# A fused local-attention, Fourier-mixing and MLP kernel on one core: global keys inside the score blocks of two batches, a second MLP in seven products from its third chunk on, and a rebuilt opening

## Chip, core and metric

The kernel runs on one core of one Trainium2 chip. The metric is device time in microseconds (us) of one execution; a kernel's time is the median of several runs. TensorE (PE) does matmuls into PSUM, VectorE (DVE) and ScalarE (ACT) drain PSUM and do elementwise work, GpSimd (POOL) does small work and issues DMAs that cast, SyncE (SP) issues the other DMAs.

## What is computed

Input q, k, v are (4 batches, 8 heads, 768 tokens, 64). Attention keeps, for each query, the local keys 0 to 95 tokens back and the 8 global keys (tokens 0 to 7), with a linear distance bias. Its output x, (4, 768, 512), goes through a Fourier mixing and a two-layer MLP:

```
scores = q k^T / sqrt(64) - slope[h] * dist     # dist = 96 for a global key out of reach
keep   = (key < 8) or (0 <= query - key < 96)
x      = softmax(scores where keep) v           # heads side by side: (4, 768, 512)
u      = x + real(fft2(x))                      # over tokens and features
un     = (u - mean(u)) / sqrt(var(u) + 1e-6)
out    = u + relu(un @ w_ch1) @ w_ch2           # 512 -> 2048 -> 512
```

## The kernel before

Work is float16 with float32 sums. Each of the four batches goes through the same stages, and the stages of different batches are interleaved on the engines.

*Attention* is done by head pair (`hp`, 4 per batch). q and k are loaded and cast by POOL's DMA queue (`load_qk`, L418), v by `load_v` (L404). In batches 0 and 1 PE transposes them (`trans`, L506, matmul L521) and DVE or ACT copies the result out (L528, L532); in batches 2 and 3 the DMA does it (`trans_dma`). `score` (L539) makes a block of scores for two blocks of 128 keys by up to 256 queries each. A head pair needs three such blocks (g = 0, 1, 2), for both heads at once, one on each half of PE's rows. In batches 0 and 1 the bias is added by PE (L565) and ACT's exp writes the weights (L599). In batches 2 and 3 each block is four matmuls with 128 output rows (L571), ACT takes the exp (L596) and DVE multiplies by a mask (`mul`, L611). The 8 global keys have a block of their own per batch (`glob`, L634, matmul L644, exp L654 into `EG`). In `av` (L665) the weights multiply V (L687); for queries beyond the second block of 128, a further matmul per head adds the global part from `EG` and a small copy `vG` of the global V rows (L680). DVE divides by the sum (`norm`, L704 and L706).

*Mixing.* DVE folds the tokens by symmetry (`fold_s`, for batch 0 `fold_0`, L803, by head pair) and the features (`fold_d`, L874); PE multiplies by tables of cosines and sines (`y_unit`, L927 into `py`; `u_unit`, L1016 into `pu`). The DVE adds x back and sums for the mean (`evac`; batch 0: `evac0`, L1038). In batches 1 to 3, x comes back in the needed token order through DRAM (`bounce`). In batch 0, PE brings it into that order with a permutation matrix, `spread` (L991): 12 matmuls of 512 columns per chunk, whose results go to PSUM in strides of four columns, in the same PSUM tile as `pu`.

*MLP.* A chunk c = 3b + pr is 256 tokens, twelve chunks in all. `centre` (L1092) makes un; PE or the DMA transposes it (`nt_unit`, L1141; `nt_dma`). `ph_unit` (L1161) is the first layer: 8 units of 16 matmuls, 256 columns each, per chunk (L1171), drained by ACT (L1177) or DVE (L1178) with the relu. The second layer has two forms. For c below CS = 8, `pg_unit` (L1193): 32 matmuls of 512 columns (L1204), two DVE drains (L1213). From CS on, `pg_units` (L1281): the chunk is taken as a 2 by 2 block product (two groups of 128 tokens, two halves of the hidden width, two halves of the output), done with seven block products instead of eight, 56 matmuls of 256 columns (L1288). For that DVE forms four sums of the hidden blocks per chunk (`s_sums`, L1248) and, once, four sums of blocks of w_ch2 (`w2_sums`, L1234), and drains the products in five steps (L1306). The products p1, p45, p6, p32, p7 wait for their sums and for each other's drains, since p1, p6, p7 share one PSUM tile and p45, p32 another.

*Order.* The order of instructions on each engine is fixed when the kernel is built, by a planner (`Plan`, L23): it keeps an estimated time per engine, and always issues the unit or operation that could start first, changed by a table of offsets (`BIAS`). All engines then work through their lists in order, waiting on semaphores. Buffers are named by tag and reused (`NBUF`): "hT", the hidden activations, has 3.

*Opening.* While the first loads run, PE does 18 warm-up matmuls (L1429). Then batch 0's attention starts; before a head pair's first score block, 4 filler matmuls are issued (`FILL`, L549).

Of the kernel before, what the change touches and what calls it, by code (L numbers as in the profile page):

```python
# [17 lines left out]
class Ring(str):  # L18

    k = 0  # L20


class Plan:  # L23
# [8 lines left out]
    LAND = {("c", "id"): 3.0, ("ld", 0): 4.8, ("ld", 1): 5.0, ("c", "dist"): 6.3, ("c", "gb"): 6.5}  # L32
    LAT = {"ACT": 0.14, "DVE": 0.12, "POOL": 0.08}

    def __init__(self):
        self.t = {"PE": 0.0, "ACT": 0.0, "DVE": 0.0, "POOL": 0.0, "SP": 0.7, "DMA": 6.0, "DMA2": 1.0}
        self.tok = {}
        self.ready = []
        self.pending = []
        self.rings = {}  # L40
        self.left = {}
        self.n = 0
        self.lanes = [0.0] * 8
        self.soft = [0.0] * 8
# [24 lines left out]
    def later(self, ways, needs=(), after=0.0, outs=(), uses=(), ring=None, lat=0.0, dma=0.0, then=None, rank=1, nd=None):  # L69

        self.n += 1
        if nd is None:
            nd = 0 if dma == 0 else 1 if ways[0][0] in ("SP", "ACT") else -1
        self.pending.append((self.n, ways, list(needs), after, outs, uses, ring, lat, dma, then, rank, nd))
        self.promote()
# [11 lines left out]
    def first(self):  # L87

        best = None
        for i, (ready, p) in enumerate(self.ready):  # L90
            if p[11]:
                ready = [max(r, self.lane(p[11])) for r in ready]
            c = (min(max(self.t[w[0]], r) for w, r in zip(p[1], ready)) - self.AHEAD * (p[10] < 0) + self.bias(p[4][0] if p[4] else None),
                 p[10], ready[0], p[0], i)
            if best is None or c < best:
                best = c
        return best
# [11 lines left out]
    def emit(self, place):  # L109
# [8 lines left out]
        if dma:  # L118
            q = "DMA2" if outs and outs[0] in (("ld", 0), ("ld", 1), ("ld", 2), ("ld", 3), ("c", "id"), ("c", "dist"), ("c", "gb")) else "DMA"
            end = self.t[q] = max(self.t[q], end) + dma  # L120
        else:
            lat += self.LAT.get(eng, 0.0)
        for o in outs:
            self.tok[o] = max(end + lat, self.LAND.get(o, 0.0)) if dma else (end + lat, eng)
        for u in uses:
            self.used(u, end + lat)
        lanes = self.lanes if nd > 0 else self.soft
        for _ in range(abs(nd)):
            lanes.append(max(end + lat, self.t[eng] + 2.2, *[self.LAND.get(o, 0.0) for o in outs]))
            lanes.pop(0)  # L130
        if ring is not None:
            self.rings[ring].append((end + lat, ring.k))
        if then is not None:
            then(end + lat)
        self.promote()

    def lane(self, nd):
        return self.lanes[nd - 1] if nd > 0 else self.soft[-nd - 1]

    narrow = False  # L140

    def pe(self, us, after=0.0, narrow=False):
        if narrow != self.narrow:
            us += 0.1
        self.narrow = narrow
# [3 lines left out]
    def slot(self, tag):  # L149
# [7 lines left out]
    BIAS = {('kG', 3): 3, (1, 2): 0.7, ('s', '*', 8): 0.3, ('mk1', '*', 2): 0.7, ('h', 1, 3): 0.3, ('v', 3, 2, 0): 6,  # L157
            ('w', '*', 1): 0.7, ('qk', 11, 0, 0): 0.7, ('ss', 1, 0): -1.5, ('ob', '*', 7): -3,
            ('qk', 14, 1, 0): -0.7, ('vGh', 3, 3): 3, (2, '*', 8): -0.7, ('vGh', 1, 3): -0.3, ('vGh', 3, 0): -0.3,
            ('xb', 12, 1): 6, ('qk', 13, 1, 0): 3, (3, '*', 1): 1.5, ('xb', '*', 2): 0.3, ('ss', 5, 1): -0.7,  # L160
            ('ss', '*', 7): -0.7, ('u', '*', 5): 0.3, (1, 5): -3, ('h', 0, 7): -3, ('ss', '*', 8): 0.7,
            ('h', '*', 2): 3, ('w2t', '*', 1): 0.3, ('qkT', 14): 1.5, ('h', '*', 10): 1.5, ('un', '*', 3): 1.5,
            ('mk1', 0): 0.3, ('un', '*', 2): -0.3, ('mk1', 5): -1.5, ('un', 5, 1): 1.5, ('ex', 2, 2, 2): -1.5,
            ('u', '*', 8): -0.7, (2, 3): -3, ('er', '*', 3): 0.7, ('qkT', '*', 2): -3, ('qk', 9, 1, 0): 3,
            ('un', 8, 1): 0.3, ('qk', 14, 1, 1): -3, (2, 56): -0.3, ('mk1', '*', 7): 0.7, (1, 86): -0.3,
            ('er', 16): 3, ('ob', '*', 10): 0.7, ('h', '*', 7): -1.5, ('ob', '*', 14): 3, ('un', 6, 1): -0.3,
            ('ex', 1, 2, 1): -3, ('unT', 0): -0.7, ('h', 0, 0): -0.7}
    AHEAD = 0.0
# [7 lines left out]
    FILL = 4  # L176
# [3 lines left out]
    def run(self, streams):  # L180

        left = [[(*u, (i, k)) for k, u in enumerate(s)] for i, (s, _) in enumerate(streams)]
        while True:
# [20 lines left out]
            if op is not None and (best is None or op[0] <= best[0]):  # L204
# [5 lines left out]
            elif not any(left) and not self.pending:  # L210
# [27 lines left out]
def kernel(  # L238
# [24 lines left out]
    DM = ()  # L263
    assert (B, H, S, Dh, NG, NL) == (4, 8, 768, 64, 8, 96)
# [18 lines left out]
    distk = np.concatenate([np.where(near < far, rel, np.where(key < NG, NL, far)), near, near[:, 0:P]], 1)  # L283
# [64 lines left out]
    NBUF = {"hT": 3, "qk": 4, "qkT": 4, "er": 2, "eg": 1, "x": 1, "xr": 1, "zy": 1, "eA": 1,  # L348
# [12 lines left out]
    dist_sb = kon.tile([P, 2, NM], FP16, tag="dist", name="dist")  # L361
    dist_k = kon.tile([P, NM], FP16, tag="distk", name="distk")
    sid = kon.tile([P, H, P], FP16, tag="sid", name="sid")
# [5 lines left out]
    W2 = {}  # L369
    mhalf = kon.tile([P, 2], FP32, tag="mhalf", name="mhalf")  # L370
    zero = kon.tile([P, 1], FP32, tag="zero", name="zero")
# [4 lines left out]
    vG = [kon.tile([P, HP, 2, 66], FP16, tag=f"vG{i}", name=f"vG{i}") for i in range(2)]  # L376

    EG = kon.tile([P, 2, 512], FP16, tag="eg", name="eg")
# [15 lines left out]
    def swq(fn, cost, needs, outs, dma, fifo=True):  # L394
        after = []
        then = None
        if fifo:
# [3 lines left out]
            then = lambda t: pl.tok.__setitem__(("sw", k), pl.t["POOL"])  # L401
        pl.later([("POOL", cost, fn)], needs + after, 0.0, outs, lat=2.2, dma=dma, rank=0, then=then)

    def load_v(b, hp):  # L404
        h0 = 2 * hp
        if b >= FB:
# [3 lines left out]
            swq(whole, 1.0, [("avdone", b - 2), ("wl", 7)], [("v", b, hp, t) for t in range(2)], 1.5, False)  # L410
            return
        for t in range(2):
# [3 lines left out]
            swq(run, 0.75, ([("avdone", b - 2), ("wl", 7)] if b > 1 else []), [("v", b, hp, t)], 0.7, b < 2)  # L416

    def load_qk(b, hp):  # L418
        n = HP * b + hp
        h0 = 2 * hp  # L420
        tag, ti = ("hT", n // 2) if n < 6 else ("qk", n - 6)
        for w, src in enumerate((q, k)):
            if b >= FB:
                for h in range(2):
# [4 lines left out]
                    swq(run, 0.75, free(tag, ti) + [("wl", 7)], [("qk", n, w, h)], 0.75, False)  # L429
# [7 lines left out]
            if n in pl.HW:  # L437
# [3 lines left out]
                pl.later([("ACT" if w else "SP", 0.45, read)], [], 0.0, [("ld", w + n)], lat=1.7, dma=1.35)  # L441
# [11 lines left out]
            swq(run, 0.82, free(tag, ti), [("qk", n, w)], 1.1)  # L453
# [13 lines left out]
    pl.users(("C",), 4 * HP + 2 + HP + len(YG) // 2 + NP + 1 - 3)  # L467
    pl.users(("D",), 4 * HP + 2 + HP + len(YG) + NP + 1)
# [16 lines left out]
    def kg_copies(b, hp):  # L485
        n = HP * b + hp

        def cp(on):
            on.tensor_copy(kG[b % 2][:, hp, :].rearrange("p (m t) -> p t m", t=2),
                           TT[n][:, 1, 0:P].rearrange("p (t m) -> p t m", t=2)[:, :, 0:16])  # L490
        pl.later([("POOL", 0.25, lambda: cp(nc.gpsimd)), ("DVE", 0.12, lambda: cp(V))], [("qkT", n)], 0.0,
                 [("kG", n)], [("free", "qkT", n)], rank=RA(b))

    def trans_dma(b, hp):
        n = HP * b + hp

        def xb(w):
            if n not in TT:
                TT[n] = buf("qkT", n, [P, 2, S], FP16, 4)
            nc.sync.dma_start_transpose(TT[n][:, w].rearrange("p (j x) -> p j x", x=P), qk16[n][:, w].rearrange("p i h d -> p (i h d)"))  # L500
        for w in range(2):
            pl.later([("SP", 1.3, lambda w=w: xb(w))], [("qk", n, w, h) for h in range(2)] + (free("qkT", n) if w == 0 else [("xb", n, 0)]), 0.0,
                     [("xb", n, w)], lat=1.7, dma=1.25)
        pl.later([("SP", 0.0, lambda: None)], [("xb", n, w) for w in range(2)], 0.0, [("qkT", n)], [("free", "qk", n - 6)])

    def trans(b, hp):  # L506
# [4 lines left out]
        src_at = ("hT", n // 2) if n < 6 else ("qk", n - 6)  # L511

        def run(start, ring):
# [9 lines left out]
            e = pl.pe(1.0, start, True)  # L523
            pl.used(("free",) + src_at, e)

            def evac():
                TT[n] = buf("qkT", n, [P, 2, S], FP16, 5)
                V.tensor_copy(TT[n], pt[:, :, 0:S])  # L528

            def evac_act():  # L530
                TT[n] = buf("qkT", n, [P, 2, S], FP16, 5)
                A(TT[n], pt[:, :, 0:S], AF.Copy)  # L532
            pl.later([("DVE", dve2(2 * S), evac)] * (n not in pl.AQ) + [("ACT", act(2 * S), evac_act)] * (b < 2), free("qkT", n), e, [("qkT", n)], CD(b, ring) * (b == 0), ring=ring, rank=RA(b))
            kg_copies(b, hp)
# [4 lines left out]
    def score(b, hp, g):  # L539
# [3 lines left out]
        def run(start, ring):  # L543
# [4 lines left out]
            for _ in range(pl.FILL if b == 0 and g == 0 else 0):  # L548
                nc.tensor.matmul(pa[:, 0, :], idn, dist_sb[:, 0, 0:512], start=True, stop=True, skip_group_check=True)  # L549
            w0, w1_ = ((256, CO), (CO, CO), (256, P))[g]  # L550
# [16 lines left out]
            for i, c0, cw in tiles:  # L567
                for s in range(2):
                    lo = 64 * s
                    if b >= FB:  # L570
                        nc.tensor.matmul(pa[:, s, c0:c0 + cw], TT[n][lo:lo + 64, 1, i * P:i * P + P],  # L571
                                         TT[n][lo:lo + 64, 0, i * P:i * P + cw], start=True, stop=True)
# [6 lines left out]
            e = pl.pe(0.27 + 0.28 * pem, start, True)  # L579
# [4 lines left out]
            def cut(t):  # L584

                if g == 1:
                    return t.rearrange("p s (i c) -> p s i c", i=2)[:, :, :, 0:CO]
# [16 lines left out]
            def mul():  # L604
                h = slice(2 * hp, 2 * hp + 2)
                o = cut(expst[hp][:, :, g * 512:g * 512 + (384 if g == 2 else 512)])
                if g == 1:
                    m = mk[:, h, 256:256 + CO].unsqueeze(2).to_broadcast([P, 2, 2, CO])
# [7 lines left out]

    def v_global(b):
        for hp in range(HP):
# [961 lines left out]
```

## Time and profile before

| | us |
|---|---|
| median of 3 runs | 256.53 (256.25 to 256.71) |
| the profiled execution | 257.17 |
| its span, first to last instruction | 255.4 |

The profile shows the one execution of 257.17 us. All times in views are microseconds from the start of its span. Busy time is the time covered by an engine's records; a matmul's record goes on past the start of the next one, so the cost of a matmul in a row of equal ones is taken from the distance of starts. In a group's row stand line, engine, operation, what is written from what, count, busy time, mean in ns of one, and the engine's idle time just before with what ended it. The windows view gives, for each stretch, its length and the busy time of PE, weight load, DVE, ACT and POOL, then the granted clock, the DMA share and GB/s.

### The profile page before, as it was taken

The page shows a single profiled execution, that of the slowest core. Times are in us where ns is not written, and L with a number is a line of the kernel's source. Part 1 is how long each engine was busy: PE and PEld are TensorE (multiplying, and loading weights), DVE is VectorE, ACT ScalarE, POOL GpSimd, SP SyncE. Part 2 cuts the span into 40 slices and gives each one's busy share as a digit, 9 for nine tenths or more (in the row PEclk, how much of TensorE's full clock was granted, in tenths as well). Part 3 has the DMA queues.
Part 4 walks back from the last instruction along what each step waited for, and adds up shares of the span by engine and source line. Part 5 has one row for each costly group of instructions (what it writes and reads, how often), then busy time and mean ns, then how long its engine had stood idle before and what let it go on. Part 6 is the DMA issues. An engine that isn't in the chain of part 4 may idle for free.

```text
span 255.4 us, 6779 instructions
## 1 busy us (share of the span) xinstructions
PE 244.0 (96%) x2838; PEld 176.2 (69%) x2838; DVE 172.0 (67%) x413; ACT 140.5 (55%) x237; POOL 89.0 (35%) x127
## 2 busy tenths in 40 slices
PE   7998687999999999999999999999999999999994
PEld 2565465498768754677794475688886577888883
DVE  4539589556995317668669879788997434674563
ACT  3477899785686321699736144953567334433200
POOL 8788734208967428556001001110022104010010
PEclk9999999999999999999999999999999999999999
DMA  7999999995999999989995704312331621130213
GB/s 197 167 165 181 276 206 175 184 167 36 167 180 194 170 172 187 220 103 81 145 124 159 201 3 123 86 41 44 129 120 42 83 41 49 53 108 0 83 47 120
DMA packets 93502, 32.11 MB, mean 126 GB/s; under 512 B 81728, under 2 KB 90048, under 8 KB 93472
## 3 DMA queue, kind: packets, MB, share of 16 engines
q0 software_dynamic: 66272, 17.06, 67.1%
q1 hardware_dynamic: 23904, 11.54, 22.5%
q10 hardware_dynamic: 3296, 3.08, 4.0%
q8 instruction: 22, 0.36, 0.6%
q14 instruction: 8, 0.07, 0.1%
HBM read 31.54 MB, written 8.65 MB: 157 GB/s over the span
## 4 chain that ended last, share of the span: by engine, by line
PE 89%; DVE 7%; ACT 2%; issue 1%; ACTq 0%
PE ph L1171 33%; PE pg L1204 22%; PE pgD L1288 6%; PE pgA L1288 4%; PE pav L687 4%; PE py L927 3%; PE pu L1016 3%; PE pz L1429 3%; PE sc L571 3%; PE pt L521 2%; ACT ex L599 2%; PE pav L680 1%; PE sc L549 1%; PE pu L991 1%; DVE qkT L528 1%; DVE x L706 1%
## 5 line engine op out<-in xcount | busy, mean ns | idle before, releaser
L1171 PE MATMUL ph<-unT,w 128*128 128x256 f16 x768 | 92.5, 273 | 0.0
L1171 PEld LDWEIGHTS <-w 128*128 128x128 f16 x768 | 72.9, 98 | 13.2 <-issue 2.5
L1177 ACT ACTIVATE hT<-ph 128x512 f16<-128x512 f32 x77 | 45.7, 598 | 46.9 <-PE ph L1171 46.5
L1204 PE MATMUL pg<-w,hT 128*128 128x512 f16 x256 | 60.4, 379 | 0.0
L1204 PEld LDWEIGHTS <-hT 128*128 128x128 f16 x256 | 24.4, 98 | 24.3 <-issue 0.9
L596 ACT ACTIVATE er<-sc 128x992 f16<-128x992 f32 (+2 forms) x24 | 21.7, 929 | 9.8 <-DVE ex L611 6.4
L599 ACT ACTIVATE ex<-sc 128x992 f16<-128x992 f32 (+2 forms) x24 | 20.7, 928 | 5.7 <-PE sc L575 5.5
L1213 DVE SCALAR_TENSOR_TENSOR u<-pg,sm,u 128x512 f32<-128x512 f32 x16 | 12.0, 747 | 14.9 <-PE pg L1204 14.8
L1117 POOL TENSOR_SCALAR sm<-sm 128x2 f32<-128x2 f32 x12 | 2.9, 242 | 53.8 <-ACT un L1110 53.8
L1110 ACT ACTIVATE un<-un 128x512 f16<-128x512 f16 x24 | 14.9, 624 | 8.3 <-DMA unT<-un 6.6
L611 DVE TENSOR_TENSOR ex<-er,mk 128x992 f16<-128x992 f16 (+2 forms) x24 | 14.7, 625 | 5.9 <-ACT er L596 5.9
L1178 DVE TENSOR_SCALAR hT<-ph 128x512 f16<-128x512 f32 x19 | 13.0, 688 | 7.8 <-PE ph L1171 7.7
L687 PE MATMUL pav<-v,ex 128*128 128x65 f16 x352 | 17.3, 193 | 0.0
L428 POOL DMA_DIRECT2D qk<-in_q_dram x16 | 13.6, 864 | 8.5 <-DMA qkT<-qk 4.8
L740 POOL DMA_INDIRECT xr<-xd,back x3 | 4.0, 1338 | 35.6 <-DVE ex L611 17.2
L687 PEld LDWEIGHTS <-ex 128*128 128x128 f16 x352 | 15.8, 97 | 0.6
L1101 ACT ACTIVATE un<-u,sm 128x512 f16<-128x512 f32 x11 | 7.8, 720 | 14.4 <-DVE sm L1083 10.0
L414 POOL DMA_DIRECT2D v<-in_v_dram x16 | 12.1, 766 | 7.2 <-DMA w<-in_moe_w_ch_dram 5.6
L428 POOL DMA_DIRECT2D qk<-in_k_dram x16 | 13.6, 862 | 1.9 <-DMA v<-in_v_dram 1.7
L680 PE MATMUL pav<-vG,eg 128*128 128x65 f16 x128 | 14.2, 193 | 0.0
L941 ACT ACTIVATE zy<-py 128x1024 f16<-128x1024 f32 (+1 forms) x13 | 10.3, 827 | 6.8 <-PE py L927 6.5
L1288 PEld LDWEIGHTS <-hT 128*128 128x128 f16 x128 | 12.5, 98 | 1.8
(152 smaller groups left out, 394.9 us busy)
## 6 DMA issues: line engine op xcount, KB each, us to landing
w<-in_moe_w_ch_dram POOLq DMA_DIRECT2D x8, 512.0 KB, 11.5
out_dram<-u SPq DMA_DIRECT2D x15, 256.0 KB
v<-in_v_dram POOLq DMA_DIRECT2D x16, 96.0 KB, 7.4
qk<-in_q_dram POOLq DMA_DIRECT2D x16, 96.0 KB, 5.4
qk<-in_k_dram POOLq DMA_DIRECT2D x16, 96.0 KB, 6.2
v<-in_v_dram POOLq DMA_DIRECT2D x8, 192.0 KB, 13.1
xr<-xd SPq DMA_DIRECT2D x3, 512.0 KB
xd<-x ACTq DMA_DIRECT2D x2, 768.0 KB
```

The lines of the kernel that those rows point to most:

```text
L428: nc.gpsimd.dma_start(qk16[n][:, w, :, h], src[b, h0 + h].rearrange("(i m) d -> m i d", m=P))
L596: A(mine(), cut(pa), AF.Exp, 0.0, 0.125)
L599: A(cut(expst[hp][:, :, g * 512:g * 512 + (384 if g == 2 else 512)]), cut(pa), AF.Exp, 0.0, 0.125)
L611: VT(o, mine(), m, op=ALU.mult)
L680: nc.tensor.matmul(o[:, s * 65:(s + 1) * 65], EG[:, s, (j - 2) * P:(j - 1) * P], vG[b % len(vG)][:, hp, s, 0:65], start=True, stop=False, ...
L687: nc.tensor.matmul(o[:, s * 65:(s + 1) * 65], lhsT, v16[b % 2][:, 2 * hp + s, i, 0:65], start=(j < 2 and a == 0), stop=(a == len(ops) - 1) ...
L1110: A(x, x, AF.Square, accum_out=MV[c][:, a, 2:3])
L1171: nc.tensor.matmul(ph[:, a * CH:(a + 1) * CH].rearrange("p (x m) -> p x m", x=2), W1[0][:, d, jb * P:(jb + 1) * P], UNT[c][:, :, d, :], st ...
L1177: pl.later([("ACT", act(512), lambda: A(dst, ph, AF.Relu)), ("DVE", dve(512), lambda: V.tensor_scalar_max(dst, ph, 0.0))], [], e, [("h", c ...
L1178: ("DVE", dve(512), lambda: V.tensor_scalar_max(dst, ph, 0.0))],
L1204: nc.tensor.matmul(pg, HT[c][:, jb, t * P:(t + 1) * P], W2[0][:, jb, :], start=(jb == 0), stop=(jb == NJ - 1))
L1288: nc.tensor.matmul(o, lhs(j), rhs(j), start=(first and j == 0), stop=(j == NK - 1), skip_group_check=True)
```

## The change

Three things change, and the planner's order with them.

1. **Global keys of batches 2 and 3.** The separate global block, its exp and its matmuls in `av` go. In a score block, the second 128 queries never use key rows 0 to 31 of that block (they are 97 or more tokens back). These 32 rows now get the scores of keys 0 to 31 of the whole sequence, and the mask keeps the first 8. To place them, each block is made from pieces of 32 keys, in PE tiles of 64 by 32 (`tile_position=(lo, 32 * a)`): 18 or 20 matmuls instead of 4. V needs the same exchange: `v_back` copies blocks 1 to 4 of V to `vB` and writes rows 0 to 31 from block 0 (POOL or DVE).

```diff
-                        nc.tensor.matmul(pa[:, s, c0:c0 + cw], TT[n][lo:lo + 64, 1, i * P:i * P + P],
-                                         TT[n][lo:lo + 64, 0, i * P:i * P + cw], start=True, stop=True)
+                        for a in range(4):
+                            for k0, q0, q1 in ([(i * P + 32 * a, 0, cw)] if a or i == 0 else [(i * P, 0, P)] + [(0, P, cw)] * (cw > P)):
+                                nc.tensor.matmul(pa[32 * a:32 * a + 32, s, c0 + q0:c0 + q1], TT[n][lo:lo + 64, 1, k0:k0 + 32],
+                                                 TT[n][lo:lo + 64, 0, i * P + q0:i * P + q1], start=True, stop=True, tile_position=(lo, 32 * a))
...
+    def v_back(b, hp):
+        def cp(eng):
+            h = slice(2 * hp, 2 * hp + 2)
+            eng.tensor_copy(vB[hp], v16[b % 2][:, h, 1:NS - 1, :])
+            eng.tensor_copy(vB[hp][0:32], v16[b % 2][0:32, h, 0:1, :].to_broadcast([32, 2, NS - 2, 66]))
...
-                        if j >= 2:
+                        if j >= 2 and b < FB:
                             nc.tensor.matmul(o[:, s * 65:(s + 1) * 65], EG[:, s, (j - 2) * P:(j - 1) * P], vG[b % len(vG)][:, hp, s, 0:65],
...
+                            w = vB[hp][:, s, i - 1, 0:65] if b >= FB and a and i else v16[b % 2][:, 2 * hp + s, i, 0:65]
```

2. **Seven products from chunk c = 2 on** (the third). For c = 2 to 7 the sums lie in memory that other stages leave free (`EG`, `vG`), one buffer each, and the third sum overwrites the second, so it waits for product 6; the first sums of a chunk wait for products of the chunk before. One sum of w_ch2 blocks is written in place in w_ch2, after the last `pg_unit` of chunks 0 and 1. "hT" has 2 buffers, and one more ("tt") is shared by loads, batch 1's x and sums of w_ch2.

```diff
-    CS = 8
+    CS = 2
+    LATE = 8
...
         def s4():
-            VT(new(2), block(0, 1), SX[c, 1], op=ALU.subtract)
+            if lean:
+                SX[c, 2] = SX[c, 1]
+                VT(SX[c, 2], block(0, 1), SX[c, 1], op=ALU.subtract)
...
+            if lean:
+                return [("sA", c - 1) if i == 0 else ("sB", c - 1)] if c > CS else [("avdone", 1), ("free", "eg", 1)]
...
+    NBUF = {"hT": 2, "tt": 1, ...
```

3. **Opening of batch 0.** The filler matmuls go. For head pairs 1 and 3 the token fold is done by PE (`fold_pe`: 32 matmuls of 128 columns with plus or minus identity as weights) and copied out by ACT or DVE. `spread` becomes a unit of its own, in plain column order, into a PSUM tile of its own, copied to u by ACT or DVE; `evac0` then adds `pu` to it. The small copies of global keys go to the engine that copies the transposed q and k. The planner gets a model of the DMA queues and a new table of offsets, so that the order of all engines changes: batch 0's attention now comes wholly ahead of batch 1's transposes, and the permutation and the two tables are loaded ahead of batch 1's q and k.

```diff
-            for _ in range(pl.FILL if b == 0 and g == 0 else 0):
-                nc.tensor.matmul(pa[:, 0, :], idn, dist_sb[:, 0, 0:512], start=True, stop=True, skip_group_check=True)
...
+        def fold_pe(hp):
+                for n, terms in enumerate(ZS):
+                    o = pf[:, n // 4, (n % 4) * P:(n % 4 + 1) * P]
+                    for x, (w, i) in enumerate(terms):
+                        nc.tensor.matmul(o, w, X[0][:, i, cols], start=(x == 0), stop=(x == len(terms) - 1))
...
-                        nc.tensor.matmul(pu[64 * h:64 * h + 64, a, :].rearrange("p (r n) -> p n r", r=4), PX[0][t, 3 * (r // 2) + jj],
-                                         X[0][t, 3 * hx + jj].rearrange("p (n r) -> p n r", r=4), start=(jj == 0), stop=False,
+                        nc.tensor.matmul(px[64 * h:64 * h + 64, a, :], PX[0][t, 3 * (r // 2) + jj], X[0][t, 3 * hx + jj], start=(jj == 0), stop=(jj == 2),
                                          skip_group_check=True, tile_position=(64 * (r % 2), 64 * h))
```

The table shows instructions that come and go, counted in both kernels.

| | before | after |
|---|---|---|
| PE: score matmuls of batches 2 and 3 | 96 | 448 |
| PE: second-MLP matmuls, 512 / 256 columns | 256 / 224 | 64 / 560 |
| PE: attention times V, global / rest | 128 / 352 | 64 / 352 |
| PE: fold / filler | 0 / 16 | 64 / 0 |
| DVE: sums of hidden blocks | 16 | 40 |
| DVE: drains of the second MLP | 37 | 55 |
| POOL / DVE: copies for `vB` | 0 / 0 | 12 / 4 |

## The prediction, made before the changed kernel was run

> **What bounds the kernel now.** I read the page first: engine shares, slices, shares of the chain.
>
> ```profile
> span 255.4 us, 6779 instructions
> ...
> PE 244.0 (96%) x2838; PEld 176.2 (69%) x2838; DVE 172.0 (67%) x413; ACT 140.5 (55%) x237; POOL 89.0 (35%) x127
> ...
> PE   7998687999999999999999999999999999999994
> ...
> DVE  4539589556995317668669879788997434674563
> ...
> DMA  7999999995999999989995704312331621130213
> GB/s 197 167 165 181 276 206 175 184 167 36 167 180 194 170 172 187 220 103 81 145 124 159 201 3 123 86 41 44 129 120 42 83 41 49 53 108 0 83 47 120
> ...
> PE 89%; DVE 7%; ACT 2%; issue 1%; ACTq 0%
> ```
>
> TensorE (PE) is 96% busy and carries 89% of the chain. Only the opening (first seven slices of 6.4 us) and the last slice are not full. So the kernel is a sum of matmul time behind an opening. The DVE row shows the danger: slices 21 to 30 stand at 7 to 9. The windows view says how much room is left there.
>
> ```profile
> 0.00:42.00 42.00, 34.70 (x654) 21.24 (x658) 27.96 (x102) 29.28 (x40) 28.38 (x45) 1.00 1.59 198
> 103.00:135.00 32.00, 32.00 (x446) 24.48 (x445) 22.38 (x43) 23.30 (x40) 11.01 (x16) 1.00 1.26 126
> 135.00:162.00 27.00, 27.00 (x187) 14.23 (x184) 23.37 (x57) 12.06 (x16) 3.08 (x5) 1.00 0.46 125
> 162.00:200.00 38.00, 38.00 (x421) 29.98 (x420) 32.37 (x63) 22.71 (x40) 5.87 (x10) 1.00 0.30 74
> ```
>
> The columns after the length are PE, weight load, DVE, ACT, POOL. From 103 to 200 us PE never idles although DVE is 70 to 87% busy; the granted clock is 1.00 throughout. In the first 42 us PE is idle for 7.3 us.
>
> **The change part by part.** Prices come from the chain in order of time, where a piece lasts from its start to that of the next.
>
> ```profile
> 8.74 0.97 PE sc L549 x4
> 10.58 0.81 PE pt L521 x24
> 47.21 1.41 PE pu L991 x12
> 81.50 0.89 PE pu L1016 x16
> 91.97 9.50 PE pg L1204 x44
> 103.68 0.38 PE ptu L1141 x32
> 105.91 0.32 PE sc L571 x4
> 106.23 1.85 PE ph L1171 x16
> 108.08 0.31 PE sc L571 x4
> 120.77 0.34 PE pgl L644 x8
> 124.67 0.27 PE sc L571 x4
> 181.00 8.73 PE ph L1171 x80
> 240.29 1.75 PE pgD L1288 x16
> ```
>
> *Second MLP.* A 512-column matmul costs 9.50/44 = 0.216 us, a 256-column one 8.73/80 = 0.109, and the seven-product code already in use (L1288) pays the same, 1.75/16. A chunk goes from 32 x 0.216 = 6.91 to 56 x 0.109 = 6.11 us; six chunks (c = 2 to 7): **-4.8 us**. Beyond its last chunk nothing hides PE, so this counts in full, if DVE keeps up (below).
>
> *Global keys.* Each switch between matmul shapes costs about 0.10 us (16 ph matmuls: 1.85 next to a score, 1.75 otherwise). Batches 2 and 3 lose one global-score block each, 0.34 plus a switch: -0.9. They also lose 64 of their 240 attention-times-V matmuls; 60 such lie between these rows of the timeline:
>
> ```profile
> 125.76 0.35 PE L687 MATMUL pav<-v,ex 128*128 128x65 f16 x6
> 127.57 1.91 PE L1171 MATMUL ph<-unT,w 128*128 128x256 f16 x16
> ```
>
> so 1.81/60 = 0.030 us each: **-1.9**. On the other side the 96 score matmuls become 448 narrow ones of 32 keys. Before, a head pair's three score blocks cost 0.32 + 0.31 + 0.27 = 0.90 us: two row halves at once, 512 columns in a row. Eight places could work at once now, so the least is the same time (+0.2 for eight pairs: 256 instead of 240 columns). But in the corner that holds the global keys two 128-column pieces follow each other on one place, and if what stands behind them waits, a block costs up to 0.12 us more: 24 blocks, +2.7. No row shows two matmuls in a row on one narrow place; I take the middle, **+1.5**.
>
> The page "TensorEngine Tiling (Array Packing)" of the Trainium skill, section Performance Considerations, speaks against the split: each matmul has an overhead of about 60 cycles, which as an estimate is 25 ns a piece and 448 x 25 ns = 11 us in all. The row L1141 above disagrees: 32 small matmuls in 0.38 us with the switch, 9 to 12 ns each.
>
> *Opening, on PE.* The 16 filler matmuls go (4 in 0.97): -3.9. The three spreads lose their strided columns; in plain order they should run like the four 496-column matmuls of the first row below, 0.24 us for each four:
>
> ```profile
> 17.48 0.40 PE L565 MATMUL sc<-dist,sid 64*64 64x496 f16 x4
> 17.72 0.38 PE L575 MATMUL sc<-qkT 64*64 64x256 f16 x8
> ```
>
> Twelve cost 0.74 instead of 1.41: -2.0. The fold of head pairs 1 and 3 on PE adds 64 matmuls at 0.89/16: +3.6. PE work in all: -4.8 - 0.9 - 1.9 + 1.5 - 3.9 - 2.0 + 3.6 = **-8.4 us**.
>
> *Opening, idle time.* These timeline rows are batch 0's path: first and last exps, the second global exp, the last attention-times-V, the first mixing matmul.
>
> ```profile
> 10.30 2.62 ACT L599 ACTIVATE ex<-sc 128x992 f16<-128x992 f32 x3 [2.54 <-PE sc L575]
> 23.42 2.56 ACT L599 ACTIVATE ex<-sc 128x992 f16<-128x992 f32 x3 [0.84 <-PE sc L575]
> 31.04 1.26 ACT L654 ACTIVATE eg<-pgl,gb 64x512 f16<-64x512 f32 x2 [0.59 <-PE pgl L644]
> 34.28 0.22 PE L687 MATMUL pav<-v,ex 128*128 128x65 f16 x2
> 42.81 1.91 PE L927 MATMUL py<-t,ww 128*128 128x256 f16 x16 [0.37 <-DVE ww L899]
> ```
>
> The exps of batch 0 ended at 25.98, but the second global exp ran at 31.04: a transpose copy and three exps of batch 1 stood ahead of it on ACT. The changed order puts batch 0's 12 exps and both global exps first, with no transpose copy between. ACT needs 4 x 2.6 + 2 x 1.26 = 12.9 us from 10.30; I allow one more for gaps, so the last attention-times-V ends near 24.7, not 34.5. From there to the first mixing matmul it was 8.5 us; two of four DVE folds go, a PE fold with its copies and a 1024-wide copy of the spread come in, and I keep the 8.5, and add 0.8 for late loads (below). The first mixing matmul comes near 34.0 instead of 42.81. Counted by the prices above, PE work ahead of it falls from 33.9 to 28.3 us (seven of batch 1's 12 score blocks, not all, stand ahead), so idle time there falls from 8.9 to 5.7: **-3.2**. Bounds: 0 (the loads hold everything) to -5. The spread's copies then crowd DVE and ACT before the first ph: +0.7 (0 to 2).
>
> Queues: on POOL's queue three tables, 0.9 MB, now stand ahead of batch 1's q and k, which come up to 5 us later by the GB/s row (slices 2 to 4, 165 to 276). PE takes their transpose ahead of the fold, near 25 us, when they land or up to 2 us before: hence the 0.8. On SP ident falls behind q, back and one vgs load; what it feeds still waits for the warm-up matmuls.
>
> *DVE.* This is what the gain is paid with. Rows by shape:
>
> ```profile
> L1261 DVE TENSOR_TENSOR mk<-hT 128x1024 f16<-128x1024 f16 x4 | 2.8, 690 | 1.0 <-ACT hT L1177 0.8
> L1306 DVE SCALAR_TENSOR_TENSOR u<-pgD,sm,u 128x512 f32<-128x512 f32 x7 | 5.3, 750 | 8.7 <-PE pgD L1288 8.7
> L1306 DVE SCALAR_TENSOR_TENSOR u<-pgA,sm,u 128x256 f32<-128x256 f32 x8 | 3.8, 480 | 2.8 <-PE pgA L1288 1.6 <-POOL sm L1118 1.1
> L1213 DVE SCALAR_TENSOR_TENSOR u<-pg,sm,u 128x512 f32<-128x512 f32 x16 | 12.0, 747 | 14.9 <-PE pg L1204 14.8
> ```
>
> Per chunk: four sums of 0.69 and 2 x 0.48 + 3 x 0.75 us of drains come, 2 x 0.75 go: +4.5, less some 0.4 by which neighbouring records overlap. Six chunks: +25 us on 172.0; the opening's edits about cancel. I summed both engines' rows over the changed order, from chunk 5's transpose to the last mixing drain of batch 3: PE 75.5 us, DVE 73.7. DVE goes from 86% (same stretch before) to **98%** of PE's time. New waits sit in its queue: the fourth sum of a chunk waits for product 6, since it overwrites that product's operand, and each chunk's first sums wait for the last chunk's products; behind them stand exps times mask, norms and mixing drains, for which PE waits. On POOL, masked copies of V wait for the previous batch's last use, with rstd and the gather behind. hT has two buffers, not three. At 98% some of this must surface; I take **+4.0 us** (0 if DVE never waits; 8, if it reaches only the 90% of its busiest slices).
>
> The sum against the profiled execution (257.17 us around a span of 255.4): -8.4 - 3.2 + 0.7 + 4.0 = -6.9, so 250.3. The runs' median, 256.53, is 0.64 below the profiled execution, so the median after: **249.6 us**.
>
> **The rivals.**
> *DVE sets the middle.* 73.7 us at 86%, what it reached before, is 85.7: 10.2 us over PE's 75.5 instead of 4, total 255.8; I put the case at 252 to 256. For: 98%. Against: at 87% in 135 to 162 us PE lost nothing.
> *The opening gives nothing:* loads hold batch 1's part, idle stays 8.9: 252.8. For: the DMA row is full up to slice 9, 57 us. Against: batch 0's own loads do not move.
> *POOL copies stop the DVE.* Six of eight V copies go to POOL:
>
> ```profile
> L963 POOL COPY rev<-zy x2: 390/393/396, 153.1 to 194.6; 128x256 f16<-128x256 f16 x2
> ```
>
> A copy of 528 elements at that rate takes 0.8 us; twelve, if each held DVE up, 9.7 us into a stage with 2 us of slack, of which my 4 us count half: 249.6 + 9.7 - 2 - 2 = 255.3. The skill's "SBUF — State Buffer", section SBUF: two separate sides, states that rule: DVE with two SBUF inputs and GpSimd share a port pair under an exclusive lock. Against: no DVE row of before is stretched next to a POOL copy.
> *Slower: handoffs.* In the seven-product chunks c = 2 to 7, PE meets four points per chunk where the next product waits for a DVE sum or drain just queued. If PE stands there for one full DVE operation, 0.75 us, 24 times, that is 18 us instead of my 4: 263.6. It decides from (6.9 + 4.0)/24 = 0.45 us a handoff on. Against: chunks 8 to 11 have the same handoffs and run without a gap, though beside a DVE at half load.
> *Narrow pieces paid one by one:* at the 0.033 us of L521, 448 cost 14.8 instead of about 6.3: 258.1.
>
> **How the numbers follow.** Forecast 0.62 (245 to 252). DVE sets the middle 0.15, opening 0.08, POOL copies 0.04, narrow pieces 0.03, handoffs 0.08. With every unknown at its good end (scores +0.2, DVE 0, opening -5) it is 242.5; I go to 244. Upwards the range takes in the opening's case and most of DVE's: 255. Left out: some 0.15 above, a few hundredths below. About 0.2% (0.5 us) is what a measurement here can tell from no change. Slower: handoffs and narrow pieces, 0.11; within: 0.02 of DVE's case; faster: the rest, 0.87.
>
> **What would show it.** First py near 34; last batch-0 pav near 25. Score blocks of batches 2 and 3: 0.31 a piece is no split cost, 0.42 the corner wait, over 0.6 the one-by-one rival. Seven products at 1.75 for 16. DVE over 90% from 110 to 190 us, with PE idle after DVE at pgA and pgD of a few us. I am wrong if PE idles over 8 us there, or if py starts after 38.

## The result, and the profile after

| | before | after | ratio, 95% interval |
|---|---|---|---|
| median of 6 runs each, one chip | 256.39 us (256.14 to 256.81) | 253.94 us (253.19 to 254.79) | 0.9907 (0.9883 to 0.9932) |
| the profiled execution / its span | 257.17 / 255.4 us | 253.83 / 252.0 us | |
| first mixing matmul (py) | 42.81 us | 39.7 us | |
| from there to the end of the span | 212.6 us | 212.3 us | |

The kernel is 0.93% faster; the forecast had 2.7%. The page of the changed kernel: busy times, then PE, DVE and granted clock in 40 slices of 6.3 us, then the shares of the chain.

```profile
span 252.0 us, 7702 instructions
...
PE 237.1 (94%) x3302; PEld 192.8 (77%) x3302; DVE 195.2 (77%) x445; ACT 139.5 (55%) x228; POOL 99.9 (40%) x137
...
PE   7783898899999999999999999979999999999994
...
DVE  2636799795889869798899989976799987646183
...
PEclk9998899999999999999999999999999999999999
...
PE 81%; DMA 6%; DVE 6%; ACT 4%; issue 1%; SPq 1%; ACTq 0%
```

PE's busy time fell by 6.9 us, but the span by 3.4 only: idle time was added. The fourth slice (19 to 25 us) stands at 3, and the clock at 8 in it and in the next. A DMA share of 6% is new in the chain. The chain in order of time (start, length, what) says which DMAs these are at the opening:

```profile
2.25 5.25 DMA ident<-idm
...
15.04 5.41 DMA vgs<-in_v_dram
20.48 0.22 DVE vG L704
20.73 0.67 DVE vG L704
21.46 0.56 DVE x L784
22.05 0.22 DVE vG L704
22.30 0.97 DVE qkT L589
23.31 0.40 PE sc L638 x8
```

and the timeline of the same kernel, in square brackets the idle time before each row and what ended it, shows who stood:

```profile
20.48 0.92 DVE L704 CAST vG<-vgs 8x128 f16<-8x128 f32 x2 [5.46 <-DMA vgs<-in_v_dram]
...
23.31 0.40 PE L638 MATMUL sc<-qkT 64*64 64x240 f16 x8 [3.67 <-DVE qkT L589]
...
30.03 0.22 PE L764 MATMUL pav<-v,ex 128*128 128x65 f16 x2
...
39.70 1.92 PE L1035 MATMUL py<-t,ww 128*128 128x256 f16 x16
...
10.97 2.56 ACT L662 ACTIVATE ex<-sc 128x960 f16<-128x960 f32 x3 [4.05 <-PE sc L638]
...
23.76 0.97 ACT L662 ACTIVATE ex<-sc 128x960 f16<-128x960 f32 x1 [3.44 <-PE sc L638]
26.27 1.26 ACT L729 ACTIVATE eg<-pgl,gb 64x512 f16<-64x512 f32 x2 [1.54 <-PE pav L756]
```

Read it from the first row on. DVE stands 5.46 us for a load of `vgs`: 4 KB, the global rows of V. The two casts after the wait belong to **batch 1** (L704); a matmul first uses what they write at 62.54 us, some 40 us later. Behind them in DVE's queue, which works in order, stand batch 0's first norm (L784) and the copy of its fourth q and k (L589). So PE waits 3.67 us, ACT 3.44, and the last attention-times-V of batch 0 ends at 30.25 instead of near 25. The load itself could not be issued earlier: all four heads' rows of a batch land in one buffer `vgs`, and batch 1's loads (L697) wait until batch 0's casts have read it, 15.0 us.

The stretches in which the forecast feared DVE (columns: length, PE, weight load, DVE, ACT, POOL, clock, DMA share, GB/s):

```profile
0.00:34.00 34.00, 26.00 (x465) 17.48 (x466) 19.38 (x73) 17.90 (x24) 25.95 (x40) 0.95 1.64 191
110.00:135.00 25.00, 24.65 (x455) 20.70 (x454) 23.02 (x46) 14.59 (x23) 11.78 (x17) 1.00 0.94 116
135.00:162.00 27.00, 26.99 (x339) 23.49 (x338) 25.84 (x62) 14.31 (x24) 6.25 (x10) 1.00 0.60 118
162.00:190.00 28.00, 26.42 (x416) 22.77 (x414) 22.68 (x41) 17.02 (x29) 2.12 (x4) 1.00 0.44 91
```

DVE is 92% and 96% busy from 110 to 162 us, near the forecast, and 81% from 162 to 190. But PE idles 0.36 us in the first two stretches, and 1.58 in the third. The waits view of PE from 40 to 250 us (total, times, longest) names that last one, and it is not DVE:

```profile
PE ph L1270 <- DMA unT<-un: 1.5, 1, 1.5
PE ptu L1240 <- ACT ex L662: 0.7, 1, 0.7
PE pav L764 <- DVE ex L674: 0.3, 1, 0.3
PE sc L626 <- DVE zy L1051: 0.2, 1, 0.2
```

### The profile page after: what moved, and what is told of

Read it like the earlier page. It is cut to its first block, busy times and chain, and to the rows that moved or that the text cites. A ratio compares the mean times of both kernels' runs of the same rounds, so it can differ in the third digit from the quotient of the medians.

```text
span 252.0 us, 7702 instructions
## 1 busy us (share of the span) xinstructions
PE 237.1 (94%) x3302; PEld 192.8 (77%) x3302; DVE 195.2 (77%) x445; ACT 139.5 (55%) x228; POOL 99.9 (40%) x137
## 4 chain that ended last, share of the span: by engine, by line
PE 81%; DMA 6%; DVE 6%; ACT 4%; issue 1%; SPq 1%; ACTq 0%
PE ph L1270 33%; PE pgD L1413 13%; PE pgA L1413 10%; PE pg L1303 6%; PE pav L764 4%; PE py L1035 4%; PE pu L1123 3%; DMA unT<-un 2%; DMA vgs<-in_v_dram 2%; PE sc L634 2%; DMA ident<-idm 2%; ACT ex L662 2%; DVE qkT L589 1%; PE pf L943 1%; PE pt L582 1%; ACT zy L1049 1%
## 5 line engine op out<-in xcount | busy, mean ns | idle before, releaser
L1413 PEld LDWEIGHTS <-hT 128*128 128x128 f16 x320 | 30.8, 98 | 4.2
L659 ACT ACTIVATE er<-sc 128x1024 f16<-128x1024 f32 (+1 forms) x24 | 22.5, 954 | 5.9 <-PE sc L634 5.0
L662 ACT ACTIVATE ex<-sc 128x960 f16<-128x960 f32 (+2 forms) x24 | 20.9, 923 | 8.1 <-PE sc L638 8.0
L1431 DVE SCALAR_TENSOR_TENSOR u<-pgA,sm,u 128x256 f32<-128x256 f32 (+1 forms) x30 | 17.1, 569 | 7.5 <-PE pgA L1413 6.6
L1431 DVE SCALAR_TENSOR_TENSOR u<-pgD,sm,u 128x512 f32<-128x512 f32 (+1 forms) x21 | 15.1, 721 | 8.5 <-PE pgD L1413 8.4
L674 DVE TENSOR_TENSOR ex<-er,mk 128x1024 f16<-128x1024 f16 (+1 forms) x24 | 15.5, 658 | 3.3 <-ACT er L659 3.3
L1287 POOL DMA_INDIRECT out_dram<-u,back x4 | 4.8, 1196 | 32.4 <-DVE u L1431 30.3
L1303 PE MATMUL pg<-w,hT 128*128 128x512 f16 x64 | 15.0, 379 | 0.0
L638 PE MATMUL sc<-qkT 64*64 64x240 f16 (+2 forms) x192 | 9.0, 260 | 4.5 <-DVE qkT L589 4.4
L784 DVE TENSOR_TENSOR x<-pav,rc 128x384 f16<-128x384 f32 x24 | 12.6, 554 | 0.6
```

What stands on the lines that cost most here:

```text
L659: A(mine(), cut(pa), AF.Exp, 0.0, 0.125)
L662: A(cut(expst[hp][:, :, g * 512:g * 512 + (384 if g == 2 else 512)]), cut(pa), AF.Exp, 0.0, 0.125)
L674: VT(o, mine(), m, op=ALU.mult)
L1303: nc.tensor.matmul(pg, HT[c][:, jb, t * P:(t + 1) * P], W2[0][:, jb, :], start=(jb == 0), stop=(jb == NJ - 1))
L1413: nc.tensor.matmul(o, lhs(j), rhs(j), start=(first and j == 0), stop=(j == NK - 1), skip_group_check=True)
L1431: V.scalar_tensor_tensor(o, x, r(t), acc, op0=ALU.mult, op1=ALU.add)
```

## The experiments

The planner lays out the whole order anew when a cost changes, so an edit could move things it does not touch. All kernels but the first therefore replay the changed kernel's order from a written list: every engine's instructions stand where they stood, except for the edit. Diffs of order show an engine's queue.

| kernel | time us | ratio to before, 95% interval | first py | span |
|---|---|---|---|---|
| c_after: the changed kernel again | 254.21 | 0.9916 (0.9888 to 0.9945) | 40.6 | 252.6 |
| e1_ident | 253.89 | 0.9893 (0.9866 to 0.9919) | 40.0 | 252.4 |
| e2_casts | 249.92 | 0.9746 (0.9720 to 0.9771) | 35.9 | 248.1 |
| e3_both | 250.01 | 0.9752 (0.9727 to 0.9777) | 35.2 | 247.7 |
| h1_loads | 249.97 | 0.9756 (0.9730 to 0.9782) | 35.9 | 247.8 |
| f4_fill | 253.17 | 0.9882 (0.9846 to 0.9918) | 39.2 | 251.4 |
| f1_wide | 249.17 | 0.9715 (0.9694 to 0.9736) | 35.9 | 247.0 |
| f2_sums | 249.11 | 0.9710 (0.9685 to 0.9736) | 35.9 | 247.4 |
| f3_unt | 248.57 | 0.9684 (0.9663 to 0.9704) | 36.0 | 246.8 |
| g1_all | 248.12 | 0.9658 (0.9637 to 0.9679) | 35.6 | 246.3 |
| g2_ex | 248.01 | 0.9668 (0.9641 to 0.9696) | 35.4 | 246.3 |
| h2_novb | 247.62 | 0.9658 (0.9632 to 0.9684) | 35.1 | 245.3 |

### The two late loads of the opening

> The changed kernel once more, as the measure for the three that run beside it. All theories: 253.9 us, about 0.991 of the kernel before; first py at 39.8 us, 5.5 us of DVE waiting for a vgs load between 15 and 20.5 us.

*ident first.* On SP:

```diff
+DMACopy ident<-idm
 DMACopy u<-in_q_dram
 DMACopy back<-backm
 DMACopy vgs<-in_v_dram
-DMACopy ident<-idm
```

> The changed kernel with its order frozen, and only the load of ident issued first on SP's queue. Theory (two small loads late in the opening): ident lands near 3.2 us as before instead of 7.5, the first transposes wait for the q cast and the warm-up matmuls (8.0 us) alone, and the whole opening moves up by 0.6 us; PE is full behind it, so the time falls to 253.3 us. Rival (the loads of the opening set its pace): first exp 0.6 us earlier, first py unchanged within 0.2 us, 253.9 us.

*Casts later.* On DVE:

```diff
 TensorCopy vG<-vgs
-TensorCopy vG<-vgs
-TensorCopy vG<-vgs
 Reciprocal rc<-pav
 TensorTensor x<-pav,rc
-TensorCopy vG<-vgs
 TensorCopy qkT<-pt
...
 TensorTensor ww<-xr
+TensorCopy vG<-vgs
+TensorCopy vG<-vgs
+TensorCopy vG<-vgs
 TensorCopy qkT<-pt
```

> The changed kernel with its order frozen, and only the three casts of batch 1's global V rows on DVE moved behind the feature fold of batch 0, some 20 us later. Theory: DVE no longer stands 5.5 us for a 4 KB load at 15 us; the copy of the fourth head pair's q and k is next limited by its transposes on PE (end near 18.8 us), so the first of its scores comes at 19.8 instead of 23.3 and first py at 36.3 instead of 39.8; PE is busy behind it, so the time falls by 3.5 us to 250.4 us. Rival A (loads set the pace): the transposes of batch 1 or the fourth head pair's data are late next, first py moves by under 1 us, over 253 us. Rival B (given back later): first py moves as in the theory, but DVE, 92 to 96% busy from 110 to 162 us, cannot follow; PE idle there grows by 2 us or more, 252.4 us or above.

> Both edits, order frozen. Theory: the two waits lie one behind the other, so the gains add: first py at 35.7 us, 249.8 us, which is the forecast that stands on record but for 0.2 us. Rival A (loads): first py at 39 or later, over 253 us. Rival B (given back in the middle by DVE): first py at 35.7, but 252 us or above.

Moving three casts that take 0.22 us each took 4.3 us off the median, a little more than expected (3.5). The timeline of e2_casts, DVE: no wait for a load, and the copy of the fourth q and k comes at 18.53 instead of 22.30.

```profile
14.80 0.27 DVE L704 CAST vG<-vgs 8x128 f16<-8x128 f32 x1
17.06 0.20 DVE L782 RECIPROCAL rc<-pav 128x6 f32<-128x6 f32 x1 [1.99 <-PE pav L764]
17.29 0.56 DVE L784 TENSOR_TENSOR x<-pav,rc 128x384 f16<-128x384 f32 x1
18.53 0.96 DVE L589 COPY qkT<-pt 128x1536 f16<-128x1536 f16 x1 [0.69 <-PE pt L582]
```

ident is another matter. It brings first py forward by 0.6 or 0.7 us in either pair, but the medians move by 0.3 us and by nothing, within the intervals. So its late load costs some tenths of a microsecond ahead of first py, and what it costs in the time is not shown. The expected sum of both edits, 249.8, came out as 250.0, since the casts alone had already given it.

*The wait, or the place in the queue?* The next kernel leaves all casts where they stand and gives batch 1's rows a buffer of their own, so that their loads are issued near 3 us.

```diff
-    vgs = kon.tile([P, 2, Dh], FP32, tag="vgs", name="vgs")
+    VGS = [kon.tile([P, 2, Dh], FP32, tag=f"vgs{i}", name=f"vgs{i}") for i in range(2)]
...
+        vgs = VGS[b]
```

> The changed kernel, order frozen, the three casts of batch 1 left where they stand in DVE's queue; only batch 1's four small loads get a buffer of their own and are issued right behind those of batch 0, near 3 us, instead of after batch 0's casts. Theory (what cost the opening is the wait for a load that was issued just before, not the casts themselves): DVE does not wait at 15 us, the casts' own 0.7 us stays on its way, first py near 36.5 us, 250.3 us. Rival (the order of the casts against norms and copies is what costs, or the loads come late whenever they are issued): DVE still stands for 3 us or more, 253 us or above.

The timeline of h1_loads:

```profile
14.79 0.61 DVE L704 CAST vG<-vgs 8x128 f16<-8x128 f32 x3
17.05 0.20 DVE L782 RECIPROCAL rc<-pav 128x6 f32<-128x6 f32 x1 [1.65 <-PE pav L764]
```

Three casts at the same place, 0.61 us, no wait, and the same 250.0 us as with the casts moved. So it was the wait for a load issued too late; the casts themselves cost nothing there, as DVE waits for PE right after them.

*Why 4.3 and not 3.5.* While PE stood, its clock fell. Windows of the changed kernel, of e2_casts and of f4_fill (granted clock is the third number from the end):

```profile
20.00:23.00 3.00, 0.00 (x0) 0.00 (x0) 2.37 (x6) 0.33 (x1) 3.00 (x5) 1.00 1.24 305
23.00:26.50 3.50, 2.85 (x46) 2.08 (x50) 3.23 (x11) 1.20 (x2) 2.56 (x4) 0.59 1.82 178
```

```profile
23.00:26.50 3.50, 2.79 (x84) 2.60 (x83) 2.15 (x8) 2.17 (x4) 3.05 (x5) 1.00 1.83 182
```

```profile
20.00:23.00 3.00, 2.97 (x17) 1.09 (x14) 2.84 (x6) 0.32 (x1) 3.00 (x5) 1.00 1.30 278
23.00:26.50 3.50, 2.52 (x62) 1.89 (x66) 3.31 (x13) 1.70 (x3) 2.99 (x4) 1.00 1.83 180
```

After 3.67 us without a matmul PE runs the next ones at 0.59 of its clock (mean of 3.5 us; 0.50 from 25 to 26.5 us). The Trainium skill has that rule, in "TensorE: Matmul & The Clock Gate", Part 1: The HAM clock gate: after an idle window of about 3.4 us the array goes to half its clock until it has been busy for such a window. This trace agrees, and f4_fill tests what it costs: fillers in the wait, all else as in the changed kernel.

```diff
+            for _ in range(15 * ((b, hp, g) == (0, 3, 1))): nc.tensor.matmul(pa[:, 0, :], idn, dist_sb[:, 0, 0:512], start=True, stop=True, skip_group_check=True)
```

> The changed kernel as it is (casts not moved), order frozen, with 15 filler matmuls of 512 columns put into the time from 19.2 to 23 us in which PE stands behind DVE's wait; they compute nothing that is used. Theory: that idle time also costs clock, in the records 0.6 to 0.9 from 20 to 30 us where the kernel with moved casts has 1.00; with the fillers the clock stays at 1.00 and the way from 23.3 us to the last attention-times-V gets 0.8 us shorter: 253.2 us. Rival (the lower clock is without cost, since ACT and DVE set the pace there): 253.9 to 254.2 us, first py unchanged.

The clock stays at 1.00. Three profiles with DVE's wait compare well, since in each of them PE starts again at 23.24 to 23.31 us: with a clock of 0.50 from 23 to 26.5 us (c_after) first py comes at 40.6, with 0.59 (the first profile of the changed kernel) at 39.7, with 1.00 (f4_fill) at 39.2. So the lower clock cost 0.5 and 1.4 us on the way to py in these executions. In the time, 253.17 us, the direction is as expected, but the interval reaches over that of the changed kernel: the 0.8 to 1.0 us there is likely, not shown.

### What the middle costs

> The kernel with the casts moved (249.9 us, 0.975 of the kernel before), order frozen, and the 448 narrow score matmuls of batches 2 and 3 taken back to 96 wide ones; this leaves the global keys out of those two batches' scores. It prices the split, for which the forecast has 1.5 us (bounds 0.2 and 2.7). Theory from the traces: the score matmuls of these batches take 6.9 us of PE where the wide ones took 6.5, so 249.4 to 249.9 us, no measurable difference. Rival (the corner wait, as forecast): 248.4. Rival (one by one): 241 to 242.

```diff
-                        for a in range(4):
-                            for k0, q0, q1 in ([(i * P + 32 * a, 0, cw)] if a or i == 0 else [(i * P, 0, P)] + [(0, P, cw)] * (cw > P)):
-                                nc.tensor.matmul(pa[32 * a:32 * a + 32, s, c0 + q0:c0 + q1], TT[n][lo:lo + 64, 1, k0:k0 + 32],
...
+                        nc.tensor.matmul(pa[:, s, c0:c0 + cw], TT[n][lo:lo + 64, 1, i * P:i * P + P],
```

The ratio falls from 0.9746 to 0.9715, by 0.0031 with some 0.0033 either way, so the split costs 0.8 us (0 to 1.6). Pieces in the chain of the changed kernel agree with the low end (x counts the records; a single block has 18 or 20 matmuls):

```profile
102.79 0.51 PE sc L634 x23
105.15 1.75 PE pgD L1413 x16
107.77 0.87 PE pgA L1413 x8
122.62 0.34 PE sc L634 x12
```

A block alone costs 0.34 us with the shape switch, two in a row 0.51: about what the wide ones cost before (0.31 and 0.32 alone). The same pieces in f1_wide read 0.33 and 0.49, so by the chain the split costs some 0.02 us a block. One by one (241 to 242) is out.

> The kernel with the casts moved, order frozen, and the four sums of hidden blocks of chunks 2 to 7 taken over 128 of 1024 columns; this leaves most of the sums out. It takes some 12 us of work from DVE between 93 and 192 us, so that DVE there falls from 90 to 96% of PE's time to some 80%. Theory (what PE's idle time in the view shows is all that DVE costs): PE is idle after DVE for 0.3 us in that stretch, so the time stays within 0.6 us of 249.9. Rival (the forecast's DVE term, 4 us, hidden in small waits): 246 to 247 us.

```diff
-            VT(new(0), block(1, 0), block(1, 1), op=ALU.add)
+            VT(new(0)[:, kk], block(1, 0)[:, kk], block(1, 1)[:, kk], op=ALU.add)
...
+        kk = slice(0, 1 if lean else NK)
```

0.9710 against 0.9746: 0.9 us, 0 to 1.8. This lies a little above the theory's 0.6 and far from the rival. The edit took 8.9 us of work from DVE between 93 and 192 us (88.2 to 79.3 us busy), not 12: from 91 to 81% of PE's time. A DVE that is 91% busy beside PE costs it about 1 us here, not 4. The drains that came with the seven products were left in, so their share is priced only by PE's waits for DVE in the view above, 0.5 us in all.

> The kernel with the casts moved, order frozen, and on SP's queue only the transposing DMA of chunk 7 issued ahead of the two output stores of chunk 5 instead of behind them. Theory: its un is ready at 157.6 us, SP issues the stores from 157.2 to 159.7 first, and PE then stands 1.4 us for the transpose at 165.1; with the transpose first it lands near 161, the wait goes, PE is full behind it: 248.5 us. Rival (the transpose waits for something else on its way): the wait stays, 249.9.

```diff
+DmaTransposeAnt unT<-un
 DMACopy out_dram<-u
 DMACopy out_dram<-u
-DmaTransposeAnt unT<-un
```

SP's timeline in e2_casts, then in f3_unt:

```profile
157.20 2.46 SPq L1531 DMA_DIRECT2D out_dram<-u  x2
159.75 1.29 SPq L1223 DMA_TRANSPOSE unT<-un  x1
```

```profile
157.78 1.23 SPq L1223 DMA_TRANSPOSE unT<-un  x1
159.11 1.01 SPq L1531 DMA_DIRECT2D out_dram<-u  x2
```

The transpose goes out 2 us earlier, PE's wait for it is gone, and 1.35 us with it (0.9746 to 0.9684: 1.6 us). No step of the forecast had this wait.

> The kernel with all three edits (248.1 us, 0.966 of the kernel before), order frozen, without the copies for vB on POOL and DVE; the weights multiply V itself, which leaves the global keys' values of batches 2 and 3 out. Theory: in the records three or four DVE operations of about 0.7 us take 1.1 beside a copy on POOL, 0.9 to 1.7 us of DVE in all, and PE does not wait for them: 247.6 to 248.2 us. Rival (the copies cost DVE what the forecast's rival gave, 5.7 us net): 242 to 244 us.

Without the copies the ratio is 0.9658, as with them (g1_all): they cost nothing that can be measured (within 0.9 us). Yet DVE and POOL do hold each other up in one place. DVE, then POOL, in the changed kernel:

```profile
130.06 0.68 DVE L1381 TENSOR_TENSOR hT<-hT 128x1024 f16<-128x1024 f16 x1
130.66 1.11 DVE L674 TENSOR_TENSOR ex<-er,mk 128x1024 f16<-128x1024 f16 x1
...
153.24 0.68 DVE L674 TENSOR_TENSOR ex<-er,mk 128x1024 f16<-128x1024 f16 x1
```

```profile
130.26 0.96 POOL L684 COPY vB<-v 128x528 f16<-128x528 f16 x1
...
133.60 0.63 POOL L684 COPY vB<-v 128x528 f16<-128x528 f16 x1 [1.35 <-PE pav L764]
```

Beside a POOL copy the multiplication by the mask takes 1.11 us instead of 0.68, and the copy 0.96 instead of 0.63; the operations that read PSUM are not stretched (131.69 to 133.0). In h2_novb, without the copies, no such multiplication takes over 0.69 us. This is the lock of the Trainium skill's page "SBUF — State Buffer", section SBUF: two separate sides, which the forecast doubted: here the trace agrees with it. Only one DVE operation of this size was stretched so, not the three or four of the expectation; two more, on two elements each, were stretched at 159 us (0.28 and 0.48 us instead of 0.17).

### All together

> The changed kernel, order frozen, with the three edits that the runs so far point to: ident's load first on SP, the three casts of batch 1 behind the feature fold, chunk 7's transposing DMA ahead of the two stores. Theory (three separate waits, PE full between them): the parts add, 4.0 for the casts, 0.3 to 0.6 for ident, 1.35 for the transpose, 248.2 us and first py near 35.2. Rival (loads of batch 1's q and k set the opening once the casts are gone, as the run of both opening edits hints): ident brings nothing, 248.6 us.

> As the kernel with all three edits, and on ACT the two halves of chunk 0's un next to each other, with an exp of batch 1 behind them instead of between. Theory: PE's wait of 0.7 us for that exp ahead of chunk 0's transpose goes, all behind it moves up: 0.5 to 0.7 us below the kernel with three edits, 247.6. Rival (the exp is late next, for the score block that waits for its PSUM bank): no difference.

g1_all, 248.12 us, ratio 0.9658 (0.9637 to 0.9679), beats both kernels: 3.4% under the one before, and by the ratio of the ratios (0.9658/0.9907, intervals apart) 2.5% under the change as it came. The parts add for casts and transpose; ident's 0.45 us beside f3_unt is within the intervals. Moving the exp as well changed nothing (248.01): its rival held. PE's wait of 0.7 us ahead of chunk 0's transpose is gone in that profile, and one of 0.8 us for an exp ahead of a score block stands in its place.

## Why the forecast was wrong, step by step

Right in direction and within the range, wrong in size: 249.6 forecast, 253.94 measured. That it fell in the range was luck, since the upper part of the range was made for late loads of batch 1 and for DVE in the middle, and neither was the cause. Against the profiled executions it is 250.3 and 253.83, 3.5 us. In spans: forecast py at 34.0 and 214.5 us behind it (248.5 in all), measured 39.7 and 212.3. So **+5.7 us ahead of first py, -2.2 behind it**.

**The step that failed** is the one on idle time of the opening: "I allow one more for gaps, so the last attention-times-V ends near 24.7" and from it py near 34. The order of ACT was read rightly: batch 0's exps do stand first. But ACT waits for PE, PE for DVE, and DVE's own queue was not walked. The last attention-times-V ended at 30.25 instead of 24.7, which is all but 0.2 us of the 5.7. In the forecast's terms, PE's idle time ahead of py, put at -3.2 us, came out at +1.0 (7.7 before, 8.6 after); and PE's busy time there fell by 4.1 instead of 5.6, as the lower clock stretched it (31.06 us, against 28.89 in e2_casts). Of the small loads the forecast says only that "what it feeds still waits for the warm-up matmuls", for ident; that batch 1's casts now stand ahead of batch 0's first norm, behind loads that wait for batch 0's casts, was to be seen in the two orders and was missed. With that wait gone (e2_casts, h1_loads) the last attention-times-V ends at 25.9 and 26.2 and py comes at 35.9; with ident first as well, at 35.2. The 3.8 us for the casts are shown. The 0.7 for ident is less sure: the four profiles with ident first have py at 35.1 to 35.6, the five in which only DVE's wait is gone at 35.9 to 36.0. The last 1.2 us (35.2 against 34.0) stay open; in e3_both the chain of the opening runs over loads of q and k, and PE stands 1.3 us for them, but nothing tested that.

The rival "the opening gives nothing" named another cause, loads of batch 1's q and k, and 252.8; the opening gave 3.1 of 8.8 us, for a cause that no rival named.

**That the opening's gain passes to the end in full** was right: from first py to the end of the span it is 212.3 us in the changed kernel, 212.2 in e2_casts and f4_fill, 211.9 in h1_loads, 212.5 in e3_both.

**Behind py** the errors were smaller and partly cancelled:

- *DVE in the middle, +4.0:* f2_sums makes it 0.9 (0 to 1.8) for the sums. The load was forecast a little too high (89% of the time and 92% of PE's from 110 to 190 us, instead of 98%), its price far too high: from 135 to 162 us DVE was 96% busy, and PE idled 0.01 us.
- *Narrow score pieces, +1.5:* 0.8 (0 to 1.6), near the lower bound.
- *Chunk 7's transposing DMA, not in the forecast:* 1.35 to 1.6 (f3_unt).
- Together 0.9 - 4.0 + 0.8 - 1.5 + 1.5 = -2.3, beside the -2.2. Each of these terms is known to 0.8 or 0.9 us only, so part of this agreement is luck.

**PE work, -8.4:** right. Busy PE is 244.0 us before, and where the clock is full, on the page of e2_casts,

```profile
PE 234.9 (95%) x3302; PEld 191.9 (77%) x3302; DVE 195.2 (79%) x445; ACT 139.2 (56%) x228; POOL 101.3 (41%) x137
```

-9.1; the changed kernel as it came has 2.2 more, all of it ahead of first py, most likely by the lower clock there (0.95 up to 34 us). 16 matmuls of the seven products take 1.75 us, as priced. Two rows of the chain settle fold (forecast 3.6) and spread (0.74 for a full twelve):

```profile
31.04 3.69 PE pf L943 x64
...
48.83 0.65 PE px L1096 x12
```

**Crowding ahead of the first ph, +0.7:** the one such wait is 0.7 us (ptu after an exp). That the size agrees is luck as far as is known: the wait is for an exp of batch 1, no run ties it to the copies of the spread, and taking it away (g2_ex) gained nothing.

**The other rivals.** DVE does not set the middle, although 253.94 lies where that rival had put the time (252 to 256): the time was lost ahead of py. Handoffs cost no 0.45 us each, since PE's waits for DVE behind py add up to 0.5. The POOL copies do stop DVE, but only three operations beside twelve copies, and nothing of it reaches the end. The forecast's own mark for being wrong, py after 38, was met.

**Small slips in the working,** none of which decides: in the DVE row it is slices 22 to 31 that stand at 7 to 9; the GB/s of slices 2 to 4 are 165 to 181, and 276 is the fifth; 10.30 + 12.9 + 1 gives 24.2, so 24.7 holds half a microsecond that is not explained; and the 8.5 us to first py are counted from the start of the last attention-times-V, 8.3 from its end.

## What to carry to other kernels

When an order is replanned, walk every in-order queue up to the first critical point and ask of each instruction not only what it costs but what it waits for: a 0.2 us cast that waits for a load holds up all that stands behind it. A buffer that is used again decides how early its next load can be issued; a second buffer of 512 bytes a partition was worth 4 us here. Busy shares do not price a wait: DVE at 91% of a full PE's time cost about 1 us in the middle, and one stop of the same engine in the opening, where it was 57% busy (up to 34 us), cost 4.

## What the hardware showed that was not expected

- A 4 KB load took 5.41 us from its issue to its landing while the DMA queues moved 193 GB/s (15.0 to 20.45 us); what held it up is not shown.
- 3.67 us of idle PE brought the clock down to 0.59 in the 3.5 us that followed (0.50 in another execution after 3.60 us); fillers in the gap kept it at 1.00.
- A copy on POOL and a DVE operation with two fp16 inputs in SBUF stretched each other, 0.68 to 1.11 us and 0.63 to 0.96; without the copies (h2_novb) no such operation was.
- 18 to 20 matmuls in PE tiles of 64 by 32 cost nearly what four wide ones cost: 0.34 us a block with the switch, against 0.33 in f1_wide.
